# The first transform of a long convolution, moved from column halves to quarters of TensorE's array

## The chip, the cores and the metric

The kernel runs on one core of a Trainium2 chip. TensorE multiplies, VectorE, ScalarE and POOL (GpSimd) work on tiles, and SyncE (SP) issues most transfers. The metric is the time of one execution on the device, in microseconds. Before the change it is 709.82 us, the median of three runs (707.43 to 710.73).

## The reference

A sequence of 2048 tokens of 640 channels goes through two sublayers, each ahead of a layer norm whose scale, shift and output gate come from a small conditioning vector. The second is an MLP of width 1728 with a squared ReLU. The first holds the change:

```python
k_shift = sum_t k_pad[:, t:t+S] * shift_k[:, ks-1-t]     # 4 taps, causal, per channel
kv = k_shift * v
y = irfft(rfft(kv, 2S) * rfft(ssm_k, 2S))[:S]             # long causal convolution, per channel
y = y + kv * ssm_D
x = x + ga * h * y                                        # h: the normed, modulated input
```

So every one of the 640 channels needs a convolution of 2048 points with its own filter, which is done as a Fourier transform of 4096 points (the signal padded with as many zeros), a product of spectra and a transform back. `ssm_D` is added to the filter's first tap.

## The kernel before

The channels are worked on in five blocks of 128 (`b` = 0 to 4), and everything is fp32. For each block the transform is split in two stages of matmuls against small tables.

The tile `p` (made by `p_tile`) holds a block's input: partition, then two planes (0 the signal `kv`, 1 the filter `ssm_k`), then 32 groups, then 64 points. A partition stands for one of 4 neighbouring channels and one of 32 stretches `n` of 64 points; a group `g` is four neighbouring channels. `load_h` and `load_x` fill it by DMA on SP, from `ssm_k` and from the buffer `kv_d` in device memory, through the views `hsrc` and `xsrc`. `skip` adds `ssm_D` to the filter's first point; for that the vector `ssm_D` lies on partitions 0, 32, 64 and 96 (channel 0 to 3 of a group, stretch 0), for block 0 in `d0`, which is loaded shifted by one channel from partition to partition, for the other blocks in `dsm`, which POOL's queue loads with four strided transfers.

`unit_a(b, i, g)` is a unit of the first transform (lines 345 to 352): for four groups it multiplies the group's 128x64 slice of `p` (stationary) with the table `cw`, 128 rows by 128 columns for the real part and as many for the imaginary part. `cw` holds the 32-point table four times on its diagonal, once for each of the four channels. The real part's matmul writes partitions 0 to 63 of a PSUM tile and the imaginary one 64 to 127, so each uses one column half of the array. Four groups fill one PSUM bank (tag `X`, four banks), and one ScalarE copy brings them to the tile `a` (`AX[b][i]`). There are 8 units for each of the two planes: 16 a block, 80 in all, each of 8 matmuls.

After that `front` (with `spectrum`, the second stage, into tiles named `h`, `x` and, for part of block 0, `eh`) multiplies the spectra on VectorE and POOL; `back` (tile `qp`) transforms back, on row halves of the array; `unit_t` transposes (tile `t`) and `unit_y` does the last stage (tile `y`), on column halves. Between them run the short convolution of the coming blocks (`kv_k`, `kv_s`, `kv_v`, `kv_m`: tiles `kt` and `vt`, `KV` or `kacc`) and the layer norm and conditioning.

The order is written by hand. A block's front has steps `FS(b, 0..9)`, and its second part has steps `GS(b, 0..17)`; a table `tab` says which piece of the other work is recorded at which step, and every engine keeps the recorded order (`keep_order`). The first units of block 0 are written out one by one at the start, between the short convolution's quarters. For block `b + 1` two units stand at step 9 of block `b`'s front, and 14 at the steps `sa` of its second part.

On TensorE an fp32 matmul of the program appears in the trace as two weight loads and two MATMULs.

## Time and profile before

| | |
|---|---|
| median of three runs | 709.82 us |
| the profiled execution | 710.85 us |
| its span, first to last instruction | 709.1 us |
| TensorE busy, share of the span | 688.2 us, 97% |
| VectorE, ScalarE, POOL busy | 336.2, 334.0, 296.2 us |
| line 350, the first transform | 1280 MATMULs, 84.6 us busy |
| line 134, the copies of its tiles | 80 on ScalarE, 47.6 us busy |
| mean granted TensorE clock | 0.996 |

The profile is that of one execution. Its page gives busy times by engine, the span in 40 slices with the busy share in tenths, the chain of work that ended last, and the costliest groups of instructions by line; PE is TensorE, PEld its weight loads, DVE VectorE, ACT ScalarE, SPq the queue of SP. In a group, "128*64" before the shapes is the part of the array that the instruction uses (rows by columns), and "x1280" is the number of instructions. The trace behind the page is asked for the busy time of each engine in a stretch of time, for the instructions in order of time, and for the chain piece by piece. In the rows in order of time the first number is the start and the second the length from the first instruction's start to the last one's end, both in us.

### The profile page before, as it was taken

What the parts mean: (1) busy time and instruction counts of PE and PEld (TensorE: products, weight loads), DVE (VectorE), ACT (ScalarE), POOL (GpSimd) and SP (SyncE); (2) the same over time, 40 slices, a digit from 0 to 9 for tenths busy, and PEclk for the clock granted to TensorE, in tenths of its full rate; (3) what the DMA queues carried; (4) which work ended last, traced back from release to release, by engine and by line L of the source; (5) the groups of instructions that cost most, each with busy time, mean ns of one, the idle gap of its engine ahead of it and who ended that gap; (6) DMA issues with size and microseconds to landing.
All of it is one profiled execution on the core that took longest, in us unless ns stands there. A gap on an engine that the chain in (4) does not pass through costs nothing.

```text
span 709.1 us, 18474 instructions
## 1 busy us (share of the span) xinstructions
PE 688.2 (97%) x7884; PEld 657.6 (93%) x7884; DVE 336.2 (47%) x662; ACT 334.0 (47%) x685; POOL 296.2 (42%) x341
## 2 busy tenths in 40 slices
PE   6898999999999999999999999999999999999997
PEld 5887899888899899889999999999999999999996
DVE  4264675775867679679831232222313313312313
ACT  3535555776874886557523323333333333233221
POOL 1061036156846968842532522422514425325213
PEclk9999999999999999999999999999999999999999
DMA  9896796869565464327320020020010100200101
GB/s 246 217 271 212 214 277 170 238 184 254 123 180 141 118 164 150 95 84 236 96 75 1 1 75 1 1 76 1 19 58 1 40 36 1 75 1 1 39 1 38
DMA packets 88840, 74.67 MB, mean 105 GB/s; under 512 B 19379, under 2 KB 74035, under 8 KB 88757
## 3 DMA queue, kind: packets, MB, share of 16 engines
q1 hardware_dynamic: 86672, 72.86, 36.4%
q8 instruction: 62, 1.02, 0.6%
q10 hardware_dynamic: 1892, 0.61, 0.4%
q14 instruction: 22, 0.17, 0.1%
q0 software_dynamic: 192, 0.01, 0.0%
HBM read 59.05 MB, written 14.42 MB: 104 GB/s over the span
## 4 chain that ended last, share of the span: by engine, by line
PE 86%; DVE 5%; DMA 4%; ACT 2%; issue 1%; POOL 1%; SPq 0%; DVEq 0%; POOLq 0%; ACTq 0%
PE acc L749 27%; PE h L679 25%; PE pa L350 9%; PE y L498 5%; PE qp L423 4%; PE x L357 3%; PE h L357 3%; PE t L487 3%; DMA p<-in_A_ssm_k_dram 2%; PE kt L226 1%; PE h L670 1%; PE vt L248 1%; PE xtp L644 1%; DVE KV L238 1%; DVE wx L139 1%
## 5 line engine op out<-in xcount | busy, mean ns | idle before, releaser
L139 POOL TENSOR_TENSOR mtmp<-mtmp 128x256 f32<-128x256 f32 x112 | 71.9, 642 | 242.5 <-ACT mtmp L711 234.6
L679 PE MATMUL h<-xt,w_S 128*128 128x256 f32 x1290 | 167.0, 281 | 0.2 <-DVE w_S L145 0.2
L679 PEld LDWEIGHTS h<-xt,w_S 128*128 128x128 f32 x1290 | 161.2, 190 | 0.4 <-DVE w_S L145 0.4
L749 PE MATMUL acc<-w_S,hring 128*128 128x320 f32 x960 | 156.8, 311 | 0.2 <-DVE hring L145 0.2
L145 DVE TENSOR_TENSOR hring<-mtmp,hring 128x256 fp32r<-128x256 f32 x112 | 64.9, 580 | 189.9 <-ACT hring L134 189.9
L749 PEld LDWEIGHTS acc<-w_S,hring 128*128 128x128 f32 x960 | 141.8, 188 | 0.7 <-DVE hring L145 0.7
L711 ACT ACTIVATE mtmp<-h,b1t 128x256 f32<-128x256 f32 x104 | 49.3, 474 | 177.1 <-PE h L679 171.6
L350 PE MATMUL pa<-wx,p 128*64 128x128 f32 x1280 | 84.6, 282 | 4.8 <-DVE p L142 2.2
L350 PEld LDWEIGHTS pa<-wx,p 128*64 128x64 f32 x1280 | 71.2, 140 | 12.0 <-issue 7.1
L134 ACT ACTIVATE hring<-mtmp 128x256 fp32r<-128x256 f32 x112 | 46.7, 417 | 46.0 <-POOL mtmp L139 44.5
L134 ACT ACTIVATE a<-pa 128x512 f32<-128x512 f32 x80 | 47.6, 599 | 33.0 <-PE pa L350 32.9
L139 DVE TENSOR_TENSOR wx<-x,wx 128x512 f32<-128x512 f32 x64 | 40.8, 681 | 19.1 <-PE x L357 9.6
L145 POOL TENSOR_TENSOR we<-wx 128x256 f32<-128x256 f32 x20 | 15.9, 794 | 76.9 <-DVE wx L139 74.9
L498 PE MATMUL y<-wx,wx 128*64 128x64 f32 x1280 | 44.6, 223 | 1.9 <-DVE KV L238 1.0
L498 PEld LDWEIGHTS y<-wx,wx 128*64 128x64 f32 x1280 | 41.3, 138 | 5.2 <-issue 2.5
L238 DVE SCALAR_TENSOR_TENSOR KV<-kt,tap,KV 128x511 f32<-128x511 f32 (+2 forms) x48 | 35.6, 742 | 19.0 <-ACT ktail L134 16.3
L142 POOL TENSOR_TENSOR wm<-wm,wm 128x640 f32<-128x640 f32 x20 | 31.8, 1588 | 28.4 <-ACT wm L311 28.3
L646 DVE TENSOR_SCALAR we<-xtp,cbs 128x256 f32<-128x256 f32 x35 | 19.0, 544 | 51.2 <-PE xtp L644 51.2
L357 PE MATMUL x<-a,gb 128*64 128x128 f32 x640 | 41.5, 273 | 0.9 <-ACT a L134 0.7
L134 ACT ACTIVATE q<-qp 128x512 f32<-128x512 f32 (+1 forms) x40 | 21.3, 583 | 37.7 <-PE qp L423 37.7
L357 PEld LDWEIGHTS x<-a,gb 128*64 128x64 f32 x640 | 35.9, 137 | 1.9 <-ACT a L134 0.9
L357 PE MATMUL h<-a,gb 128*64 128x128 f32 x512 | 34.1, 275 | 0.0
(141 smaller groups left out, 1025.1 us busy)
## 6 DMA issues: line engine op xcount, KB each, us to landing
wm<-in_w_mod_dram SPq DMA_DIRECT2D x25, 320.0 KB, 5.2
KV<-in_A_k_dram SPq DMA_DIRECT2D x20, 256.0 KB, 5.5
KV<-in_A_v_dram SPq DMA_DIRECT2D x20, 256.0 KB, 4.3
xp<-in_A_q_dram SPq DMA_DIRECT2D x5, 1024.0 KB, 9.3
out_dram<-x SPq DMA_DIRECT2D x14, 320.0 KB, 2.8
w1s<-in_B_w_dram SPq DMA_DIRECT2D x13, 320.0 KB, 3.9
w2s<-in_B_w_dram SPq DMA_DIRECT2D x13, 320.0 KB, 3.5
kv_d<-KV SPq DMA_DIRECT2D x16, 256.0 KB, 3.9
```

The costliest lines, as they stand in the source:

```text
L134: act.activation(o, i, AF.Copy)
L139: eng.tensor_mul(o, a, b)
L142: eng.tensor_add(o, a, b)
L145: eng.tensor_sub(o, a, b)
L238: dve.scalar_tensor_tensor(o, x, tap[:, b, t : t + 1], o, op0=ALU.mult, op1=ALU.add)
L350: pe.matmul(t[64 * r : 64 * r + 64, u], w, cw[:, r], start=True, stop=True)
L357: pe.matmul(t[64 * a : 64 * a + 64, s + r], gb[:, g, r, a], AX[b][i][:, 2 * g + a], start=True, stop=True,)
L423: pe.matmul(t[a][:, u], gi[l, 4 * j + u, r], w[r][l, u % 2], start=(r == 0), stop=(r == 1),)
L498: pe.matmul(y[64 * h : 64 * h + 64, 4 * (g % 2) + i], tss[g][:, i, 64 * r : 64 * r + 64], ca[:, r, h], start=(r == 0), stop=(r == 1),)
L679: pe.matmul(hps[n, f][:m], WI[1, f][:, a, b], XT[n][:, x, b], start=(b == 0 and i == 0), stop=(b == NB - 1 and i == 2),)
L711: act.activation(r[:m], h[:m], AF.Relu, bias=b1t[:m, f : f + 1])
L749: pe.matmul(acc[2 * s + i], h[:, a, s * P : (s + 1) * P], w[:, y, i * 320 : (i + 1) * 320], start=(f == 0 and ti == 0), stop=(f == NF - 1 ...
```

## The change

The first transform uses quarters of the array. A partition of `p` stands for one of two row halves `e`, one of two channels `d` and one of 32 stretches: the upper 64 partitions hold the block's first 64 channels in groups of two, the lower 64 the other 64. A matmul takes 64 rows of `p`'s slice (two channels) as stationary operand and a table of 64 columns, one of the two diagonal copies in `cw`, which is now 128x128. Row half `e` and part `r` (real, imaginary) choose the quarter of the array. A unit covers 8 groups in both row halves, 32 matmuls, and writes two PSUM banks, one for each row half; two ScalarE copies follow. There are 4 units a plane, 8 a block, 40 in all.

In the order, one new unit stands where two old ones did, or near: at the start the four filter units stand one behind each quarter of the short convolution; step 9 of a front has one unit; the second part has seven, at every second or third step. Each load of `p` is issued as two DMAs, one for each 64 partitions. `d0` is loaded shifted by 0, 1, 64 and 65 channels, and one POOL copy takes from it `dsm` for all blocks, block 0 too; the four transfers into `dsm` and its memset are gone.

```diff
-    cw = np.zeros((4, 32, 2, 32, 4))
-    for d in range(4):
-        cw[d, :, 0, :, d] = cr
-        cw[d, :, 1, :, d] = ci
-    cw = cw.reshape(128, 256)
+    cw = np.zeros((2, 2, 32, 2, 32, 2))
+    for d in range(2):
+        cw[:, d, :, 0, :, d] = cr
+        cw[:, d, :, 1, :, d] = ci
+    cw = cw.reshape(128, 128)
...
-    hsrc = ssm_k.rearrange("(g a) (n i) -> (a n) g i", a=4, i=64)
+    hsrc = ssm_k.rearrange("(b e g d) (n i) -> b e (d n) g i", e=2, d=2, g=DG, i=64)
...
     def load_h(b, n=1):
         w = DG // n
         for i in range(n):
-            sp.dma_start(
-                pt[b][:, 1, i * w : (i + 1) * w],
-                hsrc[:, b * DG + i * w : b * DG + (i + 1) * w, :],
-            )
+            for e in range(2):
+                sp.dma_start(
+                    pt[b][64 * e : 64 * e + 64, 1, i * w : (i + 1) * w],
+                    hsrc[b, e, :, i * w : (i + 1) * w, :],
+                )
...
-    def unit_a(b, i, g):
-        t = ps.tile([P, 4, 32, 4], F32, tag="X", name=f"pa_{b}_{i}_{g}", bufs=4)
-        for u in range(4):
-            w = pt[b][:, i, 4 * g + u, :]
-            for r in range(2):
-                pe.matmul(t[64 * r : 64 * r + 64, u], w, cw[:, r], start=True, stop=True)
-        o = AX[b][i][:, :, 16 * g : 16 * g + 16].rearrange("p m (u d) -> p m u d", u=4)
-        copy(act, o, t.rearrange("p u m d -> p m u d"))
+    def unit_a(b, i, q):
+        t = [
+            ps.tile([P, 8, 32, 2], F32, tag="X", name=f"pa_{b}_{i}_{q}_{e}", bufs=4)
+            for e in range(2)
+        ]
+        for g in range(8):
+            for e in range(2):
+                l = slice(64 * e, 64 * e + 64)
+                for r in range(2):
+                    pe.matmul(
+                        t[e][64 * r : 64 * r + 64, g].rearrange("p m d -> p (m d)"),
+                        pt[b][l, i, 8 * q + g, :],
+                        cw[l, r],
+                        start=True,
+                        stop=True,
+                    )
+        for e in range(2):
+            c = 64 * e + 16 * q
+            o = AX[b][i][:, :, c : c + 16].rearrange("p m (g d) -> p m g d", d=2)
+            copy(act, o, t[e].rearrange("p g m d -> p m g d"))
...
     for a in range(4):
+        off = 64 * (a // 2) + a % 2
         (pool if a % 2 else act).dma_start(
-            d0[32 * a : 32 * a + 1, 0 : D - a], ssm_D[a:D].rearrange("(o d) -> o d", o=1)
+            d0[32 * a : 32 * a + 1, 0 : D - off], ssm_D[off:D].rearrange("(o d) -> o d", o=1)
         )
+    pool.tensor_copy(dsm, d0.rearrange("p (b g d) -> p b g d", b=NB, d=2)[:, :, 0:DG, 0])
...
         elif b == 0:
-            sa = [0, 1, 2, 3, 4, 5, 10, 11, 12, 13, 14, 15, 16, 17]
+            sa = [0, 2, 4, 11, 13, 15, 17]
...
         else:
-            sa = [0, 1, 2, 3, 4, 5, 6, 7, 8, 9, 10, 11, 12, 13]
+            sa = [1, 3, 5, 7, 9, 11, 13]
```

`load_x` and the loads of block 0's filter at the start (`load_h0`) are split in the same way, and `skip` is one add of `dsm` for every block, on POOL for block 0 and on VectorE for the others.

More of the change, by code (lines that the diff above doesn't have):

```diff
@@ L158, in ssm_mlp_kernel @@
     ]
-    cw = WX[0][:, 8:10]
+    cw = WX[0][:, 8].rearrange("p (r n) -> p r n", r=2)
     ca = WX[1][:, 8:10].rearrange("p r (h n) -> p r h n", h=2)
@@ L180, in ssm_mlp_kernel @@
     dve.memset(eps_t, EPS)
-    dsm = sb.tile([P, D // 4], F32, tag="dsm", name="dsm")
-    dve.memset(dsm, 0.0)
+    dsm = sb.tile([P, NB, DG], F32, tag="dsm", name="dsm")
     tap = sb.tile([P, NB, 4], F32, tag="tap", name="tap")
-    hsrc = ssm_k.rearrange("(g a) (n i) -> (a n) g i", a=4, i=64)
-    xsrc = kv_d.rearrange("(g a) (n i) -> (a n) g i", a=4, i=64)
+    hsrc = ssm_k.rearrange("(b e g d) (n i) -> b e (d n) g i", e=2, d=2, g=DG, i=64)
+    xsrc = kv_d.rearrange("(b e g d) (n i) -> b e (d n) g i", e=2, d=2, g=DG, i=64)
     pt = {}
@@ L202, in load_x @@
         for i in range(n):
-            sp.dma_start(
-                pt[b][:, 0, i * w : (i + 1) * w],
-                xsrc[:, b * DG + i * w : b * DG + (i + 1) * w, :],
-            )
+            for e in range(2):
+                sp.dma_start(
+                    pt[b][64 * e : 64 * e + 64, 0, i * w : (i + 1) * w],
+                    xsrc[b, e, :, i * w : (i + 1) * w, :],
+                )
     def kv_load(i):
@@ L339, in skip @@
         hd = pt[b][:, 1, i0:i1, 0]
-        if b == 0:
-            add(pool, hd, hd, d0.rearrange("p (g a) -> p g a", a=4)[:, i0:i1, 0])
-        else:
-            add(dve, hd, hd, dsm[:, b * DG + i0 : b * DG + i1])
-    def unit_a(b, i, g):
-        t = ps.tile([P, 4, 32, 4], F32, tag="X", name=f"pa_{b}_{i}_{g}", bufs=4)
-        for u in range(4):
-            w = pt[b][:, i, 4 * g + u, :]
-            for r in range(2):
-                pe.matmul(t[64 * r : 64 * r + 64, u], w, cw[:, r], start=True, stop=True)
-        o = AX[b][i][:, :, 16 * g : 16 * g + 16].rearrange("p m (u d) -> p m u d", u=4)
-        copy(act, o, t.rearrange("p u m d -> p m u d"))
+        add(dve if b else pool, hd, hd, dsm[:, b, i0:i1])
+    def unit_a(b, i, q):
[13 more added lines that the diff above has]
+                        stop=True,
+                    )
+        for e in range(2):
+            c = 64 * e + 16 * q
+            o = AX[b][i][:, :, c : c + 16].rearrange("p m (g d) -> p m g d", d=2)
+            copy(act, o, t[e].rearrange("p g m d -> p m g d"))
     def spectrum(t, b, i, g, s):
@@ L799, in load_h0 @@
     def load_h0(i):
-        sp.dma_start(pt[0][:, 1, 8 * i : 8 * i + 8], hsrc[:, 8 * i : 8 * i + 8, :])
+        for e in range(2):
+            sp.dma_start(
+                pt[0][64 * e : 64 * e + 64, 1, 8 * i : 8 * i + 8], hsrc[0, e, :, 8 * i : 8 * i + 8, :]
+            )
         skip(0, 8 * i, 8 * i + 8)
@@ L817, in ssm_mlp_kernel @@
     unit_a(0, 1, 1)
-    unit_a(0, 1, 2)
-    unit_a(0, 1, 3)
     load_gb(2)
     kv_all(2)
-    unit_a(0, 1, 4)
-    unit_a(0, 1, 5)
+    unit_a(0, 1, 2)
     kv_all(3)
     load_x(0, 4)
-    unit_a(0, 1, 6)
-    unit_a(0, 1, 7)
+    unit_a(0, 1, 3)
     load_gb(3)
@@ L837, in ssm_mlp_kernel @@
         early_h(0, j)
-    def load_dsm(a):
-        pool.dma_start(
-            dsm[32 * a : 32 * a + 1, :],
-            ssm_D.rearrange("(o g a) -> a o g", a=4, o=1)[a],
-        )
     act.dma_start(ct, c.rearrange("o (b p) -> p (o b)", p=P))
     act.dma_start(ca, ca_d.rearrange("p (r h n) -> p r h n", r=2, h=2))
-    for g in range(8):
+    for g in range(4):
         unit_a(0, 0, g)
@@ L875, in ssm_mlp_kernel @@
         at(FS(b - 1, 4 if b > 1 else 8), skip, b)
-    for a in range(4):
-        at(FS(0, a), load_dsm, a)
     for j in range(2):
@@ L1069, in ssm_mlp_kernel @@
         last = b == NB - 1
-        A = [] if last else [(b + 1, i, g) for i in (1, 0) for g in range(8)]
+        A = [] if last else [(b + 1, i, g) for i in (1, 0) for g in range(4)]
         def next_a(b=b, A=A):
-            if len(A) == 16:
+            if len(A) == 8:
                 ab_start(b + 1)
@@ L1081, in ssm_mlp_kernel @@
                 next_a()
-                next_a()
             if j % 2 and j >= 3:
```

## The prediction

> **What bounds the kernel now.** I read the page's totals and slices first, then the groups, then the busy times by stage, then single stretches of TensorE's timeline, and last the chain of waits up to 57 us.

> ```profile
> PE 688.2 (97%) x7884; PEld 657.6 (93%) x7884; DVE 336.2 (47%) x662; ACT 334.0 (47%) x685; POOL 296.2 (42%) x341
> PE   6898999999999999999999999999999999999997
> DVE  4264675775867679679831232222313313312313
> ACT  3535555776874886557523323333333333233221
> PE 86%; DVE 5%; DMA 4%; ACT 2%; issue 1%; POOL 1%; SPq 0%; DVEq 0%; POOLq 0%; ACTq 0%
> L350 PE MATMUL pa<-wx,p 128*64 128x128 f32 x1280 | 84.6, 282 | 4.8 <-DVE p L142 2.2
> L134 ACT ACTIVATE a<-pa 128x512 f32<-128x512 f32 x80 | 47.6, 599 | 33.0 <-PE pa L350 32.9
> L498 PE MATMUL y<-wx,wx 128*64 128x64 f32 x1280 | 44.6, 223 | 1.9 <-DVE KV L238 1.0
> ```

> TensorE is busy for 97% of the span and makes up 86% of the chain; the edited line, L350, has 84.6 us of it. All of that lies in the first 16 of the 40 slices (17.7 us each), where VectorE and ScalarE stand at 5 to 8 tenths. Behind it, from about 309 us, is the MLP, which the edit leaves alone. So TensorE is what the edit can shorten, but the two other engines are close behind, and that has to be priced by stage.

> ```profile
> core 0: us, PE busy (x) PEld busy (x) DVE busy (x) ACT busy (x) POOL busy (x), PEclk, DMA share, GB/s
> 62.40:93.00 30.60, 30.60 (x546) 26.79 (x546) 19.16 (x48) 19.78 (x36) 0.00 (x0) 1.00 0.72 207
> 120.30:153.20 32.90, 32.06 (x554) 27.93 (x552) 23.17 (x52) 25.87 (x46) 9.29 (x6) 1.00 0.79 215
> 180.50:211.70 31.20, 29.76 (x540) 26.93 (x540) 26.69 (x52) 25.64 (x54) 19.67 (x14) 1.00 0.53 150
> 237.30:263.60 26.30, 26.18 (x506) 23.42 (x508) 20.67 (x41) 23.66 (x52) 20.69 (x14) 1.00 0.66 170
> ```

> These are the four stretches (blocks 0 to 3) in which the inverse transform of one block runs between the first transform of the next. 14 of each block's 16 units stand there.

> **The price of a unit.** An fp32 matmul of the program is two weight loads and two MATMULs in the trace. A unit before has 8 matmuls, 16 MATMULs of 128 columns. A unit after has 32 matmuls, 64 MATMULs of 64 columns, and does the work of two old units; there are 40 for 80.

> ```profile
> 29.05 7.21 PE L350 MATMUL pa<-wx,p 128*64 128x128 f32 x128 [1.69 <-DMA p<-kv_d]
> 43.07 2.06 PE L423 MATMUL qp<-we,gi 64*128 64x128 f32 x32
> 209.53 1.28 PE L320 MATMUL mc<-ones,wm 128*128 128x1 f32 x10
> 298.20 3.02 PE L498 MATMUL y<-wx,wx 128*64 128x64 f32 x96
> ```

> Take the last MATMUL's length off each stretch and divide by the starts before it. pa: (7.21 - 0.28)/127 = 54.6 ns from start to start. y: (3.02 - 0.22)/95 = 29.4 ns. qp, two row halves: (2.06 - 0.28)/31 = 57.4 ns. mc uses the whole array, moves one column and still takes some 115 ns, so 115 ns is what it costs to load 128 columns of weights. qp loads 128 columns too and has twice the rate: two row halves load and multiply side by side. y loads 64 columns into two column halves: if one such load is half of 115, some 58 ns, then 29.4 ns each says that two column halves work side by side as well. Both divisions are shown, each alone; the four quarters together are not shown by any row.

> Lower end: four quarters at once, 58.8 ns for a round of four MATMULs, 64/4 x 58.8 = 0.94 us a unit. Upper end: no more in flight than the trace has, 64 x 29.4 = 1.88 us. Two old units cost 32 x 54.6 = 1.75 us. I take 0.94: qp and y are the nearest rows, and they differ from the new unit only in that it does both divisions at once. So 40 x (1.75 - 0.94) = 32.4 us of TensorE work goes; at the other end 5.2 us is added.

> A change of the array's division costs time too:

> ```profile
> 243.22 0.66 PE L487 MATMUL t<-ident,q 128*128 128x128 f32 x4
> 243.80 1.09 PE L350 MATMUL pa<-wx,p 128*64 128x128 f32 x16
> 244.73 1.10 PE L498 MATMUL y<-wx,wx 128*64 128x64 f32 x32
> 245.66 1.04 PE L350 MATMUL pa<-wx,p 128*64 128x128 f32 x16
> 246.63 0.55 PE L487 MATMUL t<-ident,q 128*128 128x128 f32 x3
> ```

> From t to t 3.41 us. At the rates above pa is 2 x 0.87, y 0.94 and the four transposes, at about 0.11, 0.44: 3.12. The rest, 0.29, is two changes, 0.14 each. pa to y and back costs none, since both use two column halves. After, a unit shares its division with nothing. In the built programs' order the stretches of one division on TensorE go from 155 to 169, so 14 x 0.14 = 2.0 us comes back. Net, 30.4 us less for TensorE.

> **What lies beside other work.** Copies: still 80 of 128x512 on ScalarE, the same bytes, nothing gained or lost in sum; but both copies of a unit now come after its last matmul, and hold two of the four X banks.

> - 62 to 93 us: 14 old units (12.2) become 7 (6.6), two changes fewer: 5.9 less, 24.7 us against 19.8 of ScalarE, which works in bursts. I keep 4.0.
> - 120 to 153: 5.6 less, about four changes more: 5.0. That would be 27.9 us against 25.9 of ScalarE, 93%. I keep 3.3.
> - 180 to 212: 5.0 would give 26.2, under VectorE's 26.7, which held TensorE up once already, by the 0.97 us of the first row below. I keep 2.2.
> - 237 to 264: 5.0 would give 21.3, under ScalarE's 23.7, so at most 2.6. I keep 1.7.
> - The unit at step 9 of each front, 0.8: kept whole for block 1, half for block 3, none for block 2, where VectorE is late from a load of 11.80 us (last row of the chain below); block 0's is in the next part. 1.3.

> ```profile
> 194.79 1.15 PE L498 MATMUL y<-wx,wx 128*64 128x64 f32 x32 [0.97 <-DVE KV L238]
> ```

> ```profile
> 11.53 3.83 PE pa L350 x48
> ...
> 16.38 1.90 PE pa L350 x32
> ...
> 20.01 2.37 DVE kacc L238 x6
> ...
> 23.20 2.51 DMA kv_d<-kacc
> ...
> 29.05 7.22 PE pa L350 x128
> ...
> 56.94 2.68 PE pa L350 x32
> ...
> 159.08 11.80 DMA p<-in_A_ssm_k_dram
> ```

> The start, 0 to 62 us. The last k transposes stand behind six old units before and behind three new ones after; the 5.7 us of pa between 11.5 and 18.3 become two new units, 1.9. The chain goes on over VectorE's kacc, some 3.1 us a quarter (20.01 to 23.2) and back to back by then, which leaves about 1.5 of the 3.8. The new copy of dsm goes on POOL ahead of the first skip, for which the first unit waits: that unit comes some 0.3 us later (an old add on POOL of 128x8 and this copy of 128x160 are both short), and the kacc chain, which has VectorE for its limit, hides it; uncovered it costs the 0.3. The four loads of dsm go off POOL's queue in the front of block 0, and its memset off VectorE: I cost both at nothing, and without cover they could only gain.

> ```profile
> 25.86 2.99 SPq L203 DMA_DIRECT2D p<-kv_d  x4
> 62.53 1.08 ACT L134 ACTIVATE q<-qp 128x512 f32<-128x512 f32 x2 [2.27 <-PE qp L423]
> ```

> Each load of p is two halves now, 38 issues on SP for 19, where a whole one took 0.75 us of its queue (2.99 for four). The first unit needs both halves, 0.4 us more if a half costs half; the last of eight is issued 3 us later than the last of four if a half costs as much as a whole. The four units then take 0.94 and eight copies of 0.54 (1.08 for two), 5.3 us where 7.22 and one copy of 0.60 stood: 2.5 less, if no load holds them. 1.5 + 2.5 - 0.4 = 3.6; I give 1.3 up to late halves and keep 2.3. At 56.94 one new unit takes 0.94/1.75 of the 2.68: 1.2 less. 3.5 us, between 1 and 5. Elsewhere the second halves are issued well ahead of use.

> **Sum.** 3.5 + 4.0 + 3.3 + 2.2 + 1.7 + 1.3 = 16.0 of the 30.4 us. The profiled execution took 710.85 us (span 709.1), so 694.9; the median shown, 709.82, is 1.0 lower. I forecast 695. If nothing but the start and the first stretch counts, 7.5, it is 703; if nearly all of it counts, 27, it is 684.

> **The rivals.** *Two at a time.* In the program the two passes of a quarter's matmul stand together, ahead of the next quarter's. If a pass waiting for its own quarter keeps the third and fourth from starting, a unit is 1.88 us: +5.2 and +2.0, with no cover, as TensorE is the bound: 718. It decides above (69.9 - 2.0)/2560 = 26.5 ns a MATMUL. For it: no stretch has starts closer than 29.4 ns on average. Against it: qp and y both overtake such a wait for a second tile.

> *Starts are rationed.* A MATMUL and its load cost a fixed slot whatever the tile. Then y's 29.4 may be the slot and not the load. A slot between 22, the middle of 14.7 (four at once) and 29.4, and 26.5 ns takes off 11.6 to 0 us of TensorE work and, by the share kept above, 6 to 0 of the time: 705 to 711, I say 707. [...]

> *The cover is gone everywhere.* ScalarE and VectorE set the pace in all four stretches; then only the start counts, about 707 with its 3.5. Against it: TensorE has no idle time at all between 62 and 93, and the waits on VectorE are in 180 to 212 alone.

> **How the numbers follow.** Four quarters at work, 684 to 703: 0.76. Rationed or covered, 703 to 711: 0.10. Two at a time, 714 to 720: 0.13. Dearer still, 0.01. Half a per cent, 3.5 us, is about what the runs can tell: faster (under 706.3) 0.82, same 0.05, slower 0.13. The range that leaves out two in ten is 683 to 708.

> **What would show it.** L350's group: 2560 MATMULs, 40 to 55 us busy; over 75 us is two at a time. Four units in a row near 27 us taking 4 to 5.5 us. TensorE's idle time before L498, L423 and L357 up, ended by ACT and DVE: the 14 us that I don't keep. ACT's 80 copies near 47.6 us. The prediction is wrong if a quarter of the array waits for its neighbours, if the half loads of 64 partitions land later than whole ones, or if ScalarE's bursts eat more than half.

## The result

The changed kernel takes 716.04 us (median of 12 runs, 711.10 to 719.01), the kernel before 710.10 (12 runs, 707.43 to 711.92): 1.0078 times, with an interval of 1.0052 to 1.0104. I had forecast 695.0, so the time is 21 us above the forecast and the sign is wrong. The profiled execution of the changed kernel took 715.55 us, span 713.8; before it was 710.85 and 709.1.

The page of the changed kernel, totals, slices, the clock, the two groups of the edit and the transfers' queue:

```profile
PE 670.7 (94%) x9164; PEld 639.8 (90%) x9164; DVE 332.9 (47%) x661; ACT 330.8 (46%) x685; POOL 295.1 (41%) x338
PE   5798989989889989999999999999999999999997
PEclk9889999999999999999999999999999999999999
q1 hardware_dynamic: 108480, 72.86, 39.7%
L354 PE MATMUL pa<-wx,p 64*64 64x64 f32 x2560 | 52.8, 230 | 12.4 <-DMA p<-kv_d 3.4
L134 ACT ACTIVATE a<-pa 128x512 f32<-128x512 f32 x80 | 43.6, 601 | 26.9 <-PE pa L354 26.8
```

The first transform did become cheaper on TensorE, 52.8 us busy for 84.6. But TensorE as a whole fell by only 17.5 us, and its idle time rose from 709.1 - 688.2 = 20.9 to 713.8 - 670.7 = 43.1 us: nothing of the saving reached the end. The granted clock falls under nine tenths in the second and third slice. The stretches that answer to the four of the prediction, in the changed kernel:

```profile
core 0: us, PE busy (x) PEld busy (x) DVE busy (x) ACT busy (x) POOL busy (x), PEclk, DMA share, GB/s
63.30:93.50 30.20, 26.50 (x780) 23.10 (x778) 19.74 (x50) 18.80 (x36) 0.00 (x0) 1.00 0.71 202
...
122.50:155.20 32.70, 27.99 (x776) 23.90 (x776) 20.56 (x52) 25.54 (x48) 9.34 (x6) 1.00 0.93 227
...
184.80:216.90 32.10, 26.84 (x778) 23.77 (x780) 27.01 (x52) 25.69 (x54) 20.04 (x14) 1.00 0.58 155
...
242.50:268.50 26.00, 24.07 (x746) 21.20 (x748) 20.66 (x41) 23.18 (x52) 20.66 (x14) 0.93 0.67 174
```

Each is about as long as before (30.6, 32.9, 31.2, 26.3), with 2 to 5 us of TensorE idle in it. What it waits for shows in its rows in order of time:

```profile
21.70 7.13 PE L369 MATMUL eh<-a,gb 128*64 128x128 f32 x96 [1.09 <-ACT a L134]
...
33.69 1.16 PE L354 MATMUL pa<-wx,p 64*64 64x64 f32 x64 [1.08 <-DMA p<-kv_d]
36.05 1.98 PE L354 MATMUL pa<-wx,p 64*64 64x64 f32 x60 [1.20 <-DMA p<-kv_d]
39.02 1.98 PE L369 MATMUL x<-a,gb 128*64 128x128 f32 x16 [0.99 <-ACT a L134]
...
92.28 0.85 PE L354 MATMUL pa<-wx,p 64*64 64x64 f32 x42 [0.87 <-issue]
...
119.10 1.16 PE L354 MATMUL pa<-wx,p 64*64 64x64 f32 x64
...
177.88 0.49 PE L435 MATMUL qp<-we,gi 64*128 64x128 f32 x4 [1.69 <-POOL we L145]
...
206.96 0.34 PE L354 MATMUL pa<-wx,p 64*64 64x64 f32 x8 [0.98 <-issue]
```

Four things are to be seen. The row at 119.10 is an undisturbed unit: (1.16 - 0.23)/63 = 14.8 ns a MATMUL, so four quarters do work at once. At 33.69 and 36.05 the unit waits for its half loads. At 21.70 the same 96 MATMULs take 7.13 us that took 5.46 before, and at 39.02 sixteen take 1.98 for 1.09: half clock. The trace records half clock from 21.8, 35.5 (twice as long), 93.5, 178.8 and 260.8 us on, in stretches of 3.41 us, six in all against one before (58.0); both executions have one more at the very end. And at 92.28 and 206.96 TensorE stops in the middle of a unit for which everything is there: "issue" means that the trace shows no semaphore that held it.

The load of block 3's filter, which holds up VectorE's `skip`, first in the kernel before, then in the changed one (rows of VectorE in order of time):

```profile
170.90 0.21 DVE L142 TENSOR_TENSOR p<-p,dsm 128x32 f32<-128x32 f32 x1 [4.76 <-DMA p<-in_A_ssm_k_dram]
```

```profile
175.22 0.22 DVE L142 TENSOR_TENSOR p<-p,dsm 128x32 f32<-128x32 f32 x1 [7.13 <-issue]
```

Its wait grew from 4.76 to 7.13 us, and the wait of `qp` at 177.88 and the half clock from 178.8 are what follows. The second row names no semaphore, but in the trace the load's second half lands at 175.15 us, just ahead of it. SP's rows for the issue of this load, first before, then after the change, show where the lateness begins:

```profile
159.08 4.68 SPq L195 DMA_DIRECT2D p<-in_A_ssm_k_dram  x1
```

```profile
160.53 7.20 SPq L196 DMA_DIRECT2D p<-in_A_ssm_k_dram  x2
```

The two halves hold SP's queue for 7.20 us where the whole load took 4.68. The second half's issue begins at 163.46 us, and 11.7 us later it lands, as the whole load did 11.8 us after its own.

So there were four suspects: A, the half loads; B, the coarse unit, which holds two banks and copies late; C, the half clock; and D, the stops behind no semaphore. E, the prediction's own rival, is that the other engines set the pace anyway.

### The profile page after: what moved, and what is told of

It reads as the page before. It is cut to its first block, busy times and chain, and to the rows that moved or that the text cites. A ratio compares the mean times of both kernels' runs of the same rounds, so it can differ in the third digit from the quotient of the medians.

```text
span 713.8 us, 21055 instructions
## 1 busy us (share of the span) xinstructions
PE 670.7 (94%) x9164; PEld 639.8 (90%) x9164; DVE 332.9 (47%) x661; ACT 330.8 (46%) x685; POOL 295.1 (41%) x338
## 4 chain that ended last, share of the span: by engine, by line
PE 63%; DVE 6%; POOL 3%; ACT 2%; issue 2%; POOLq 0%; DVEq 0%
PE acc L761 26%; PE h L691 25%; PE y L510 2%; PE h L369 1%; PE qp L435 1%; PE x L369 1%; PE h L682 1%; DVE KV L240 1%; PE xtp L656 1%; DVE KV L139 1%; DVE up L139 1%; PE t L499 1%; PE gr L1032 1%; POOL xp L142 1%; ACT KV L468 1%
## 5 line engine op out<-in xcount | busy, mean ns | idle before, releaser
L134 ACT ACTIVATE hring<-mtmp 128x256 fp32r<-128x256 f32 x112 | 46.7, 417 | 45.9 <-POOL mtmp L139 44.3
L354 PEld LDWEIGHTS pa<-wx,p 64*64 64x64 f32 x2560 | 46.2, 143 | 20.8 <-issue 7.4
L354 PE MATMUL pa<-wx,p 64*64 64x64 f32 x2560 | 52.8, 230 | 12.4 <-DMA p<-kv_d 3.4
L134 ACT ACTIVATE a<-pa 128x512 f32<-128x512 f32 x80 | 43.6, 601 | 26.9 <-PE pa L354 26.8
L510 PE MATMUL y<-wx,wx 128*64 128x64 f32 x1280 | 46.7, 226 | 7.0 <-ACT wx L134 4.2
L369 PE MATMUL x<-a,gb 128*64 128x128 f32 x640 | 43.4, 281 | 1.0 <-ACT a L134 1.0
L142 POOL TENSOR_TENSOR wm<-wm,wm 128x640 f32<-128x640 f32 x20 | 31.9, 1596 | 25.7 <-ACT wm L313 25.6
L240 DVE SCALAR_TENSOR_TENSOR KV<-kt,tap,KV 128x511 f32<-128x511 f32 (+2 forms) x48 | 35.5, 739 | 14.9 <-ACT ktail L134 13.4
L369 PEld LDWEIGHTS x<-a,gb 128*64 128x64 f32 x640 | 37.7, 141 | 1.7 <-ACT a L134 1.2
L134 ACT ACTIVATE q<-qp 128x512 f32<-128x512 f32 (+1 forms) x40 | 21.3, 583 | 35.2 <-PE qp L435 35.2
## 6 DMA issues: line engine op xcount, KB each, us to landing
p<-in_A_ssm_k_dram SPq DMA_DIRECT2D x8, 512.0 KB, 12.2
```

Of the source, the lines that this page charges most:

```text
L134: act.activation(o, i, AF.Copy)
L142: eng.tensor_add(o, a, b)
L240: dve.scalar_tensor_tensor(o, x, tap[:, b, t : t + 1], o, op0=ALU.mult, op1=ALU.add)
L354: pe.matmul(t[e][64 * r : 64 * r + 64, g].rearrange("p m d -> p (m d)"), pt[b][l, i, 8 * q + g, :], cw[l, r], start=True, stop=True,)
L369: pe.matmul(t[64 * a : 64 * a + 64, s + r], gb[:, g, r, a], AX[b][i][:, 2 * g + a], start=True, stop=True,)
L510: pe.matmul(y[64 * h : 64 * h + 64, 4 * (g % 2) + i], tss[g][:, i, 64 * r : 64 * r + 64], ca[:, r, h], start=(r == 0), stop=(r == 1),)
```

## The experiments

Ratios are to the kernel before, run on the same chip beside each (its medians there were 710.3 to 710.7 us).

**Whole loads in the changed kernel.** The channels go back to the old order (four neighbours to a group), so one transfer fills all 128 partitions; units, places and table stay.

```diff
-    hsrc = ssm_k.rearrange("(b e g d) (n i) -> b e (d n) g i", e=2, d=2, g=DG, i=64)
+    hsrc = ssm_k.rearrange("(g a) (n i) -> (a n) g i", a=4, i=64)
...
-            for e in range(2):
-                sp.dma_start(pt[b][64 * e : 64 * e + 64, 1, ...], hsrc[b, e, :, ...])
+            sp.dma_start(pt[b][:, 1, ...], hsrc[:, ...])
...
-            o = AX[b][i][:, :, c : c + 16]...
+            o = AX[b][i][:, :, 32 * q : 32 * q + 32]...("p m (g e d) -> p m g e d")[:, :, :, e]
```

> The changed kernel with each load of p whole again, 128 partitions in one transfer (the channel order of the kernel before); quarter units, places and table stay. Theory A, the half loads land late and TensorE's waits for them cost the gain: the waits on p<-kv_d between 29 and 37 us go, x of block 0 starts before 37 us (39.0 with halves), the load of h for block 3 lands some 2.3 us earlier; 706 to 711 us. Theory B, the coarse unit (two banks held, two copies behind its last matmul) and the other engines eat the gain: 714 to 717, as the changed kernel's 716.0.

Measured: 712.52 us, ratio 1.0031 (1.0006 to 1.0056). The half loads cost the changed kernel about 3.5 us; without them it is still not faster than the kernel before. Both theories miss the number; A explains part.

**Half loads in the kernel before.**

```diff
-            sp.dma_start(pt[b][:, 1, ...], hsrc[:, ...])
+            for e in range(2):
+                l = slice(64 * e, 64 * e + 64)
+                sp.dma_start(pt[b][l, 1, ...], hsrc[l, ...])
```

> The kernel before, with nothing but its loads of p split into two of 64 partitions. Theory A: slower by 3 to 7 us, 713 to 717, with TensorE waiting for p<-kv_d near 29 us and more stretches at half clock. Theory B: within 1.5 us of the kernel before, 709 to 711.5.

Measured: 716.74 us, 1.0103 (1.0069 to 1.0137). Alone they cost the kernel before 6.3 us (four executions), about as much as the whole change. VectorE's wait for block 3's filter is 7.85 us there.

**Coarse units in the kernel before.**

```diff
-    def unit_a(b, i, g):            # one bank, 8 matmuls, one copy
+    def unit_a(b, i, q):            # two banks, the 16 old matmuls, then both copies
...
-            sa = [0, 1, 2, ..., 13]
+            sa = [1, 3, 5, 7, 9, 11, 13]        # the changed kernel's places
```

> The kernel before, with its units in pairs: the matmuls of two old units, then both copies, at the places of the changed kernel; loads, matmuls and TensorE's rate as before. Theory A: within 2 us of the kernel before, 709 to 712. Theory B: slower by 4 us or more, 714 and up, with TensorE waiting for banks (released by VectorE's KV or ScalarE's a) near L354's work.

Measured: 713.25 us, 1.0045 (1.0023 to 1.0068). Between the two theories: 2.8 us. This run and the one with whole loads differ in the matmuls of a unit, in `dsm`'s one copy, and in the stride at which a copy writes `a`: a copy takes 639 ns on the mean there and 600 here. So the faster unit, by which the first transform's 81 us of TensorE here come down to 53 there, was worth about 713.25 - 712.52 = 0.7 us, and the intervals of the two overlap. The stride may hide a little of it, as it may of the 3.5 us above; what it costs alone no run shows.

**Spare matmuls against half clock,** in the changed kernel.

```diff
+        spin(t[0]..., n)     # n matmuls of 128x128x128 into the unit's own bank, overwritten after
         for g in range(8):
```

> The changed kernel with spare matmuls (their result is overwritten or never read) put ahead of the instructions for which TensorE waits near 19, 21, 29 to 39, 91 and 258 us, so that it is busy in those waits. Theory C, half clock after the waits is itself a good part of the loss: no more than two of the six stretches at half clock stay, the eh group near 21.7 us takes 5.5 instead of 7.1 us, and the time is 711 to 713. Against it, the stretches at half clock lie where another engine or a load sets the pace anyway: 715 to 717 though the clock is full.

Measured: 723.82 us, 1.0191 (1.0156 to 1.0226), 7.8 us worse than without. The eh group did run at full clock, but five stretches of half clock stayed where at most two were to, the spare work itself arrived late, and the stops behind no semaphore grew (TensorE in order of time):

```profile
25.47 3.49 PE L382 MATMUL eh<-a,gb 128*64 128x128 f32 x58 [1.05 <-issue]
...
38.51 2.50 PE L371 MATMUL pa<-ident 128*128 128x128 f32 x10
...
141.18 1.33 PE L357 MATMUL pa<-wx,p 64*64 64x64 f32 x37 [2.52 <-issue]
```

At 38.51 ten spare MATMULs stand ahead of a unit that then starts without a wait; at 141.18, where nothing was added near, TensorE stands still for 2.52 us inside a unit. So this run prices nothing about the clock, but it pointed at the stops. In the changed kernel they are these, by its view of waits (engine, line, what ended the wait: us in total, times, longest):

```profile
PE pa L354 <- issue: 2.4, 3, 1.0
...
PE y L510 <- issue: 1.6, 3, 0.7
...
PE kt L228 <- issue: 0.7, 1, 0.7
```

The kernel before has none. The trace's record of transfers has a queue for instructions with packets of 16 KB, and each of the seven stops ends soon after the start of one: a packet at 14.26 us and work again at 17.11, 89.81 and 92.28, 134.56 and 137.03, 140.11 and 142.51, 187.94 and 190.48, 204.79 and 206.96, 209.17 and 211.51, 2.2 to 2.9 us from one to the other.

**Bursts.** Behind the last block of the kernel before: 24 units' worth of quarter matmuls, then column-half matmuls of 64 and 128 columns, all on one constant tile.

```diff
+    burst_q(24)          # 1,536 MATMULs, quarters of 64x64
+    burst_c(64, 64)      # 1,024 MATMULs, column halves, 64 columns
+    burst_c(32, 128)     # 512 MATMULs, column halves, 128 columns
```

> The kernel before, and behind its last block bursts of matmuls on one constant tile, with hardly a transfer beside them: 1,536 MATMULs in four quarters of 64x64, 1,024 of 64 columns in two column halves, 512 of 128 columns in two column halves. Theory D: the quarters stop about once in 128 MATMULs (16 KB of instructions with their weight loads) and take 18 ns or more a MATMUL on the mean against 14.8 without stops, or keep 14.8 here, where the fetch has no traffic beside it, if it is the traffic that makes it late; the two others run through at about 29 and 55 ns. Against theory D: 14.8 throughout would leave the stops in the kernel to the loads around them, or to something else.

Measured (TensorE in order of time, and the instruction queue's line of the page):

```profile
711.46 2.09 PE L1240 MATMUL bq<-ident 64*64 64x64 f32 x128 [1.40 <-issue]
715.20 2.09 PE L1240 MATMUL bq<-ident 64*64 64x64 f32 x128 [1.65 <-issue]
718.95 2.09 PE L1240 MATMUL bq<-ident 64*64 64x64 f32 x128 [1.65 <-issue]
...
746.49 58.84 PE L1253 MATMUL bc<-ident 128*64 128x64 f32 x1536
```

```profile
q8 instruction: 86, 1.41, 0.8%
```

The quarters run 128 MATMULs in 2.09 us, (2.09 - 0.23)/127 = 14.6 ns each, and then stop for 1.65 us, again and again. The period is 3.74 us: 29.3 ns a MATMUL on the mean. The queue carried 86 packets for the 62 of the kernel before, 24 more for 3,072 MATMULs and as many weight loads, so by this count a packet holds 256 instructions, 128 MATMULs with their weight loads. The two kernels' pages give about the same: 62 packets for 2 x 7,884 before, 254 each, and 72 for 2 x 9,164 in the changed kernel, 255 each. This is with the transfers all but silent (6% of the DMA engines' time), so the traffic isn't the cause. Column halves run through without a stop at all. But those of 64 columns, at the 29.4 ns of `y` in the prediction, use up a packet in 128 x 29.4 ns = 3.76 us: by that estimate they stand just at the pace at which packets came for the quarters.

**Few instructions, the same quarters.** Whole loads; the 64 MATMULs of a unit become 8 of 512 columns. The transform is left out.

```diff
-        for g in range(8):
-            for e in range(2):
-                for r in range(2):
-                    pe.matmul(t[e][64 * r : 64 * r + 64, g], pt[b][l, i, 8 * q + g, :], cw[l, r], ...)
+        for e in range(2):
+            for r in range(2):
+                pe.matmul(t[e][64 * r : 64 * r + 64], pt[b][l, i, 8 * q, :], pt[b][l, i, 8 * q : 8 * q + 8], ...)
```

> [...] Theory D, TensorE's instructions run out: no stop inside a unit, and 704 to 708. Theory E, the other engines and the loads set the pace: 710 to 713, and TensorE's idle time is ended by VectorE, ScalarE and loads.

Measured: 701.03 us, 0.9881 (0.9843 to 0.9919, four executions), 11.5 us under the run with whole loads, which it differs from in this alone. Totals, the group, and TensorE in order of time:

```profile
PE 663.6 (95%) x6924; PEld 602.5 (86%) x6924; DVE 336.6 (48%) x661; ACT 331.4 (47%) x685; POOL 295.2 (42%) x338
L351 PE MATMUL pa<-p 64*64 64x512 f32 x320 | 47.3, 647 | 9.7 <-DMA p<-kv_d 5.0
```

```profile
176.85 1.09 PE L351 MATMUL pa<-p 64*64 64x512 f32 x8
177.87 1.15 PE L508 MATMUL y<-wx,wx 128*64 128x64 f32 x32
...
181.66 1.09 PE L351 MATMUL pa<-p 64*64 64x512 f32 x8 [1.62 <-DVE KV L255]
184.65 1.15 PE L508 MATMUL y<-wx,wx 128*64 128x64 f32 x32 [1.90 <-DVE KV L238]
```

A unit takes TensorE about as long as with quarters of 64 columns (1.09 us), every stop that is left ends with a semaphore, and the time drops, below even the 704 to 708 that D gave. So D is right, and E, with its 710 to 713, is not. How the 11.5 us come about is shown in part: in the two profiled executions, 8.8 us apart in span, the whole-load run has stops of 2.16, 0.62 and 0.56 us of this kind, 3.3 together, and eight stretches of half clock for five, each worth up to 1.7 us (half of its 3.41). That the three more come from those stops is shown for one of them at most: the half clock from 35.25 us follows the stop that ends at 34.94. Weight loads became fewer too; against them as the cause stands the burst, where 128 with all their weight loads run at 14.6 ns.

**Light units that weren't.** Three runs were to take TensorE time away in the column halves or over the whole array, with MATMULs of 512 columns (the transform is left out): in pairs at the changed kernel's places, in the old fine units, and in fine units over the whole array. The second one's edit:

```diff
-            for u in range(4):
-                for r in range(2):
-                    pe.matmul(t[64 * r : 64 * r + 64, u], pt[b][:, i, 4 * g + u, :], cw[:, r], ...)
+            for r in range(2):
+                pe.matmul(t[64 * r : 64 * r + 64]..., pt[b][:, i, 4 * g, :], pt[b][:, i, 8 * (g // 2) : 8 * (g // 2) + 8]..., ...)
```

> The kernel before with its units in pairs at the changed kernel's places, each pair's 32 matmuls replaced by four of 512 columns (they leave out the transform, what they multiply is meaningless): about the quarter units' TensorE time, some 0.9 us for a pair, with a sixteenth of their instructions. Theory D, quarter units lose their gain to TensorE running out of instructions (it stands still inside a unit, behind no semaphore, and goes on some 2.4 us after the start of a 16 KB instruction packet): no such stop, and under 708 us, 4 or more below the 712.5 with quarter units and whole loads. Theory E, the other engines and the loads set the pace once TensorE has less to do: 710 to 714.

> The same light matmuls in the kernel before's own single-bank units and places (the transform is left out). If a third less TensorE time in the first transform is worth what I predicted, 694 to 699 us. Theory B, the coarse unit is what eats it: 4 us or more below the light pairs. Theory E: within 2 us of the kernel before, 708 to 712.

> The kernel before with each unit's 16 MATMULs replaced by two of 512 columns over the whole array (the transform is left out): half the TensorE time of a unit, 0.43 us for 0.87, single banks, whole loads, old places. If half the TensorE time of the first transform is worth what I predicted: 692 to 698. Theory B, it is worth something where units stay fine: 698 to 706, well under the pairs. Theory E: 707 to 711, with TensorE idle where it was busy.

Measured: 711.24 us, 1.0021 (1.0000 to 1.0041); 711.21, 1.0005 (0.9990 to 1.0021); 707.54, 0.9955 (0.9936 to 0.9975). The group of the first and of the last:

```profile
L353 PE MATMUL pa<-p 128*64 128x512 f32 x320 | 78.4, 615 | 5.6 <-DVE p L142 2.2
```

```profile
L347 PE MATMUL pa<-p 128*128 128x512 f32 x160 | 85.7, 641 | 7.4 <-DMA p<-kv_d 3.5
```

I had mis-sized them, by estimates that no row of a trace had shown: 78.4 and 85.7 us busy are about what the old units take (84.6). So these runs don't say what less TensorE time is worth in fine units, and that stays open. They are controls of another kind: at the old TensorE time, far fewer instructions change 0 to 3 us (713.25 to 711.24 in pairs). The kernel before isn't short of instructions: none of its stops up to 309 us ends behind no semaphore. And the run with few instructions in quarters differs from the pairs here, beside `dsm` and the copies' stride (644 ns a copy for 600), only in TensorE's time for a unit: 711.24 to 701.03 for 78.4 - 47.3 = 31 us. So about a third of what TensorE saves comes through in coarse units, when instructions don't run short.

**Cut loads instead of half loads,** in the kernel before: each load in two along the groups, over all 128 partitions.

```diff
     def load_h(b, n=1):
+        n = 2 * n
```

> The kernel before with each load of p cut in two along the groups instead of the partitions: as many transfers as with half loads, each over all 128 partitions. If it is the number of transfers in SP's queue that makes half loads late, 714 to 717 us as with half loads (716.7); if it is that they cover 64 partitions only, 709 to 712.

Measured: 709.35 us, 0.9988 (0.9977 to 1.0000). So it is not the number of transfers. The line of the loads' queue and the line of the 512 KB loads, first with half loads in the kernel before, then with cut ones:

```profile
q1 hardware_dynamic: 108480, 72.86, 39.3%
```

```profile
p<-in_A_ssm_k_dram SPq DMA_DIRECT2D x8, 512.0 KB, 12.3
```

```profile
q1 hardware_dynamic: 108480, 72.86, 36.5%
```

```profile
p<-in_A_ssm_k_dram SPq DMA_DIRECT2D x8, 512.0 KB, 9.6
```

As many packets and bytes, but 39.3% of the engines' time for 36.5%, and a filter's load lands 12.3 us after its issue for 9.6. In the packets' records the 41,600 of 256 bytes take 27 ns each (median) over 64 partitions and 18 over 128; the two shares, of spans of 717.5 and 706.4 us, differ by 9.3 ns for each of them. Why, no run here shows.

**Two attempts at a faster kernel.** The changed kernel with cut loads over 128 partitions:

> The changed kernel with loads over all 128 partitions, each cut in two along the groups (what took 1.3 us off the kernel before). If the loads' sizes help here as there: 710 to 712, level with the kernel before; if the quarter units' stops decide: 712 to 714.

Measured: 709.97 us, 0.9991 (0.9971 to 1.0011): level. And quarters for blocks 0 and 1 only, the old fine units for the rest, cut loads (the quarters' table is gathered from the wide one by two VectorE copies):

```diff
+        quarter = b == 0
-            unit_a(*A.pop(0))
+            (unit_q if quarter else unit_a)(*A.pop(0))
```

> Loads over all 128 partitions, cut in two along the groups; quarter units for blocks 0 and 1 only (the start and the first inverse transform, where the run with cut loads and quarter units throughout, at 710.0, was 4 to 6 us ahead of the kernel before until 93 us), the old fine units with the wide table for blocks 2 to 4 (where that run gave 2 us back). If the instruction supply decides, the lead stays: 704 to 707 us, 0.5 to 0.9% under the kernel before. If the lead there comes from chance in the loads, or the later stretches are late anyway: 708 to 711.

Measured: 707.79 us, 0.9979 (0.9957 to 1.0000). It is the fastest here that leaves nothing out, 2.5 us under the kernel before, but its interval touches no difference, and it missed the 704 to 707 that I expected. In its first inverse transform a unit waits 1.09 us for a cut load (82.11) and another 2.39 us for a bank that VectorE's KV holds (88.75), so the coarse unit is part of what is left.

## Why the prediction was wrong

The same points of the program, and how far each run is ahead (-) or behind (+) the kernel before there, in us, by the starts of TensorE's rows in the profiled executions (the run with few instructions has whole loads too):

| point | before at | changed | whole loads | few instructions |
|---|---|---|---|---|
| first eh | 21.90 | -0.20 | -2.46 | -3.51 |
| first x, block 0 | 36.94 | +2.08 | +0.30 | -1.57 |
| first t, block 0 | 63.95 | +1.03 | -0.11 | -2.87 |
| first h, block 1 | 93.06 | 0.00 | -0.61 | -7.27 |
| first t, block 1 | 121.78 | +1.63 | +0.31 | -8.06 |
| first h, block 2 | 153.25 | +1.95 | -0.35 | -9.34 |
| first t, block 2 | 181.03 | +4.23 | -0.71 | -9.93 |
| first h, block 3 | 211.72 | +5.18 | +0.43 | -9.80 |
| first t, block 3 | 237.31 | +5.19 | +0.79 | -8.78 |
| first h, block 4 | 263.61 | +4.92 | +0.06 | -10.57 |

**The unit's price** was right: 0.94 said, 1.09 from a unit's start to the next work, of which 0.14 are the change of division. "Two at a time" is out, although 716.0 lies among its 714 to 720: inside a unit a MATMUL starts every 14.8 ns. And 52.8 us busy lies in the 40 to 55 that I named.

**The step that failed is the sum's first: the saving per unit was taken from the rate inside a unit, as if the instructions for it were always there.** 64 MATMULs in 0.95 us where 32 took 1.75 is a 3.7-fold demand for instructions, and the change part by part counted matmuls, weight loads, copies and transfers, but not the bytes of the program. In the burst a quarter MATMUL cost 29.3 ns on the mean, not 14.6; in the kernel, where units stand between other work, the shortage took 11.5 of the 12.2 us that quarters without it give over the coarse units (713.25 to 701.03). The rival "starts are rationed" had the price of this, 22 to 26.5 ns and 705 to 711 us, but as a slot for every MATMUL, and I gave it too little. Such a slot the burst's trace doesn't show, with 14.6 ns for 128 in a row. Its 29.3 ns on the mean come from its stops, one in 128 MATMULs, as many as a packet holds by the count above.

**The start** (3.5 kept, 1 to 5): -1.0 in place of it. The eh group, which was to gain from the chain on VectorE, did so with whole loads (2.5) and hardly with halves (0.2). For late halves I took off 1.3; they cost 1.8 at the first x (39.02 against 37.24 with whole loads). Half clock behind the waits cost 1.67 us on the eh group and about 1.6 on the first x and eh. I had no term for the clock anywhere, though the prediction's rows show it at 56.94 (2.68 us for 32 MATMULs that take 1.97 elsewhere).

**"Elsewhere the second halves are issued well ahead of use",** priced at nothing: wrong. For block 3's filter the first half's issue held SP's queue, so that the second half was issued 4.4 us later on the clock than the whole load before; it holds VectorE up for 2.4 us more (7.13 for 4.76), and the 2.3 us lost between the first h of block 2 and the first t of block 2 go with this. With the start this makes up the 3.5 us of the half loads.

**62 to 93 us** (4.0 kept): 1.0 in the changed kernel, 4.4 with few instructions. The size was right for the work, and the stops and a wait for a bank (1.54 us at 90.85) took it. **120 to 153** (3.3): -0.3, and 1.3 with few instructions; ScalarE's copies of `wx` there end a wait of 2.92 us (152.85), so the cover was thinner than the busy share said. **180 to 212** (2.2): -1.0, and -0.1 with few instructions: VectorE's and POOL's order of work sets this stretch whatever TensorE saves. The rows at 181.66 and 184.65 above show it, two waits on VectorE's KV. "The cover is gone" holds here alone. **237 to 264** (1.7): 0.3, and 1.8 with few instructions: right for the work. **Step 9** (1.3): with few instructions 0.8 in block 1, 0.6 in block 2, and 1.0 lost in block 3. The changed kernel lost 1.6 in block 1, where the half clock from 93.5 us alone costs 1.6, lost 2.3 in block 2 by the late load, and won nothing in block 3.

So of the 16.0 us kept, some 9 were there without the shortage and the half loads (701.0 against 710.3); the kept shares were too high by some seven, and two costs that I had at zero or 1.3, instructions and half loads, took 11.5 + 3.5. From run to run: 710.5 + 2.8 (coarse units) - 12.2 (quarters) + 11.5 (instructions) + 3.5 (half loads) = 716.1. These are differences of the runs' medians one after the other, so that the sum closes by itself; it shows the sizes and proves nothing more.

**The rest.** ScalarE's 80 copies take 43.6 us; `dsm` in one copy cost nothing that shows. That TensorE's idle time would be ended by VectorE, ScalarE and late halves came true; that it could be ended by nothing visible wasn't in the list.

## What to carry over

Before a matmul is cut into smaller tiles of the array, count its instructions a microsecond, not only its columns: here quarter matmuls, which used up 256 of them in 2.09 us, stopped for 1.65 us of every 3.74, with the DMA engines busy for 6% of the time. Keep a load over all 128 partitions, and if it must be cut, cut it along the free dimension: in the kernel before half loads cost 6.3 us and loads cut along the groups none (709.35 for 710.7). And where TensorE's waits grow, look at the granted clock behind them: a wait of 1.1 us (ahead of the eh group) was followed by 1.7 lost to half clock (7.13 us for 5.46).
